# Turning q, k and x on TensorE, off-diagonal keys as tiles of their own, and a written-out order, in a local attention and low-rank mixer kernel

## The chip, the cores and the metric

The kernel runs on one core of one Trainium2 chip. The metric is the device time of the core in microseconds (us), of one launch. Engines are named as in the profile: PE is TensorE's matmul stream, PEld its weight loads, ACT is ScalarE, DVE is VectorE, POOL is GpSimd, and SP issues transfers. In the profile, L967 means line 967 of the kernel file.

## What is computed

There are 4 batches of 8 heads, 768 positions and 64 channels. Queries see the 8 first keys and the last 96 keys up to themselves, with a linear penalty on the distance; the heads' outputs, side by side, are x (768 by 512), which a low-rank mixing of the positions and an MLP then use:

```python
scores = scale * np.matmul(q, k.transpose(0, 1, 3, 2)) + bias   # local band and 8 global keys
a = np.exp(scores - max); a = a / (a.sum(-1) + 1e-09)
x = np.matmul(a, v)            # heads side by side: (4, 768, 512)
xt = x.transpose(0, 2, 1)
h = xt @ U @ V                 # U: 768 x 32, V: 32 x 768
u = x + h.transpose(0, 2, 1)
ch = np.maximum(u @ w_ch1, 0.0) @ w_ch2     # 512 -> 2048 -> 512
return u + ch
```

## The kernel before

**Units of work.** Heads go in pairs: pair p = 4b + hp holds heads 2hp and 2hp + 1 of batch b, so there are 16 pairs. `attention(p)` (L584) makes the tasks of one pair, `mlp(b)` (L952) those of one batch. Each task is one or a few instructions on one engine, with an estimated duration, the tasks that it needs, and the buffers that it takes and gives back. A planner (`Planner.run`, L159) walks through simulated time and always starts the ready task with the smallest priority number; the numbers are in a table `PRIO` or come from the place in the program. The result is one fixed order per engine. For a PE task that waits on another engine the planner keeps a `margin` (0.15 to 1.3 us) beyond the estimated latency.

**A pair.** Loads `lk`, `lq`, `lv` (L453, L457, L461; issued from POOL, cast to fp16 on the way; for pair 0, k and q come from SP in fp32 and are cast). For pairs 0 to 6 (`by_pe`) q and k are turned on PE by `TK` and `TQ` (`tr`, L600: 12 products of 64 columns each, with the identity, two column tiles at a time) and brought out of PSUM by `EK` and `EQ`. For pairs 7 to 15 `EK` and `EQ` are DMA transposes, issued from SP (`dtr`, L624). `KO` copies the 32 first keys of kT behind each block, so that a slice of 128 columns starting 32 further on is the off-diagonal key block; `VO` and `VG` build the fitting v blocks `vo` (shifted by 32 partitions, for most pairs by a transfer from SP, L651, then a copy on POOL, L368). `SB` puts the bias in PSUM (first batch only, L689: identity times a scaled bias), `S` makes the scores in products of 64 rows, two heads side by side in the array (L708), `EX` the exponential (L735), `MK` multiplies by a mask (batches 1 to 3), `PV` (L804, L805) multiplies by v, `RC` and `NM` divide (L839, L843), `XC` casts x to fp16 (L869).

**The mixing.** `UP` (`mixed`, L773) turns x by six products with the identity (L778) and makes U^T x by six products with u16 as the stationary operand (L788); `TE` copies the second to SBUF (L902), `HM` adds V times it in PSUM (L911; for batches 1 to 3 in two half arrays of 64 rows), and `E0`/`E1` bring out uT (L364). For pairs 12 to 15 (`XT`) x is turned by a DMA transpose (L880) instead of L778, and added on DVE. The other route, with x as the stationary operand (`xu`, tasks `XE` and `XU`), is in the code but no pair uses it.

**The MLP.** `M1a`/`M1b` (L967) are the first product: 16 units per batch, each 4 chunks (one per pair of the batch) by 2 halves of 384 columns; the first three chunks are `M1a`, the last `M1b`. The units go in turn through two pairs of PSUM banks, which `RL` (ReLU on ACT, L984) gives back. The second product uses seven products in place of eight (L1047, tasks `P1` to `P7`), with sums `PA`, `PB`, `TWa`, `TWb` on DVE; `RS` (L1035) adds the low-rank part in half arrays; `DI` to `DH` (L1060, L1083) add up, and SP stores (L1091).

**Order.** Attention of batch b + 1 runs between the products of batch b, in all phases. POOL issues all loads in its order, with at most 8 under way; SP issues stores, `vo` transfers and DMA transposes in its order. L1118 fills PE's idle time before the first M1 with products of zeros, to hold the clock.

Of the kernel before, what the change touches and what calls it, by code (L numbers as in the profile page):

```python
# [16 lines left out]
PE, ACT, DVE, POOL, SP = "PE", "ACT", "DVE", "POOL", "SP"  # L17


PRIO = {  # L20
# [244 lines left out]
def kernel(  # L265
# [13 lines left out]
    nc = tc.nc  # L279
# [888 lines left out]
```

## Time and profile before

| | |
|---|---|
| runs (us) | 232.76, 232.97, 234.19; median 232.97 |
| profiled execution: span, first to last instruction | 231.3 us |
| profiled execution: its own time | not given apart; the median of the runs lies 1.7 us above the span, the lowest run 1.5 us |
| first M1 product starts / last product's result reaches DVE | 35.09 us / 227.47 us |
| PE busy | 223.4 us (97%) |
| DVE, ACT, POOL busy | 153.1, 118.7, 90.2 us |
| granted TensorE clock | 1.000 |

A group line of the profile reads: line, engine, operation, what is written and read, shapes, count, then busy time, mean ns of one, and the idle time of the engine just before these instructions with what ended it. A matmul's mean is its length from issue to the end of its results, and they overlap: what one costs in a stream is the distance from one start to the next. The chain of waits is the work that ended last, followed back to the start.

### The profile page before, as it was taken

How to read it: one execution, taken by the hardware profiler on the slowest of the kernel's cores; microseconds unless marked ns; L12 is line 12 of the kernel's file. 1: busy time of each engine (PE TensorE's matmuls, PEld its weight loads, DVE VectorE, ACT ScalarE, POOL GpSimd, SP SyncE). 2: the span in 40 equal slices, each digit the busy share in tenths (PEclk: the TensorE clock that was granted, in tenths of full speed). 3: DMA queues.
4: the chain of work that ended last, by engine and by line, in shares of the span. 5: the costliest groups of instructions: out<-in, count | busy, mean ns of one | idle time of the engine just before them, and what ended most of it. 6: DMA issues, size and time to landing. Idle time of an engine off the chain costs nothing.

```text
span 231.3 us, 5732 instructions
## 1 busy us (share of the span) xinstructions
PE 223.4 (97%) x2402; PEld 158.3 (68%) x2402; DVE 153.1 (66%) x321; ACT 118.7 (51%) x161; POOL 90.2 (39%) x116
## 2 busy tenths in 40 slices
PE   7889999999999999999999999999999999999993
PEld 2556675565788885656678885666689875658882
DVE  6548772499987975375867785395888840626762
ACT  3576978878632446766652228868610025662000
POOL 9789968349929960264800911030100000000000
PEclk9999999999999999999999999999999999999999
DMA  7999999999999999992961995221020630000025
GB/s 169 162 163 150 156 189 211 207 188 166 167 157 160 175 166 235 219 123 22 130 56 41 162 162 173 56 41 30 15 22 17 157 136 4 0 0 3 0 84 191
DMA packets 89642, 26.96 MB, mean 117 GB/s; under 512 B 77040, under 2 KB 86640, under 8 KB 89616
## 3 DMA queue, kind: packets, MB, share of 16 engines
q0 software_dynamic: 63616, 13.24, 69.3%
q1 hardware_dynamic: 26000, 13.35, 27.3%
q8 instruction: 19, 0.31, 0.5%
q14 instruction: 7, 0.06, 0.1%
HBM read 27.46 MB, written 6.29 MB: 146 GB/s over the span
## 4 chain that ended last, share of the span: by engine, by line
PE 84%; POOL 7%; DMA 6%; issue 1%; ACT 0%; DVE 0%; POOLq 0%
PE ps L967 37%; PE ps L1047 33%; PE ps L708 4%; DMA vt<-in_v_dram 3%; DMA stgk<-in_k_dram 3%; PE ps L805 2%; PE ps L788 2%; POOL vo L368 2%; PE ps L804 2%; PE ps L1035 1%; POOL stgk L453 1%; POOL vt L461 1%; PE ps L778 1%; PE ps L911 1%; POOL stgq L453 1%
## 5 line engine op out<-in xcount | busy, mean ns | idle before, releaser
L967 PE MATMUL ps<-uT,w 128*128 128x384 f16 x512 | 88.1, 326 | 0.3 <-ACT uT L364 0.3
L967 PEld LDWEIGHTS <-w 128*128 128x128 f16 x512 | 48.1, 98 | 32.2 <-issue 1.0
L984 ACT ACTIVATE htr<-ps 128x768 f16<-128x768 f32 x64 | 51.9, 811 | 32.4 <-PE ps L967 32.2
L735 ACT ACTIVATE ep<-ps 128x1024 f16<-128x1024 f32 (+1 forms) x48 | 44.1, 952 | 16.0 <-PE ps L708 15.9
L1047 PEld LDWEIGHTS <-htr 128*128 128x128 f16 x384 | 36.1, 98 | 6.5 <-issue 2.0
L1047 PEld LDWEIGHTS <-sA 128*128 128x128 f16 x288 | 27.5, 98 | 3.8 <-issue 0.5
L461 POOL DMA_DIRECT2D vt<-in_v_dram x16 | 16.5, 1031 | 34.4 <-PE ps L805 27.9
L748 DVE TENSOR_TENSOR ep<-ep,mask 128x1024 f16<-128x1024 f16 x24 | 16.6, 691 | 16.4 <-ACT ep L735 16.4
L1060 DVE TENSOR_TENSOR x_sb<-ps,x_sb 128x256 f32<-128x256 f32 x48 | 19.9, 421 | 9.9 <-PE ps L1047 9.4
L1047 PE MATMUL ps<-w,htr 128*128 128x256 f16 x192 | 24.5, 273 | 0.0
L1047 PE MATMUL ps<-tB,htr 128*128 128x256 f16 x192 | 24.4, 273 | 0.0
L1047 PE MATMUL ps<-w,sA 128*128 128x256 f16 x192 | 24.4, 273 | 0.0
L368 POOL COPY vo<-vt 32x650 f16<-32x650 f16 x22 | 18.1, 823 | 9.5 <-DMA vt<-in_v_dram 8.9
L1001 DVE TENSOR_TENSOR sA<-htr 128x768 f16<-128x768 f16 x16 | 9.5, 594 | 18.3 <-ACT htr L984 18.1
L364 ACT ACTIVATE u<-ps 128x256 f32<-128x256 f32 x12 | 4.6, 384 | 29.7 <-PE ps L1047 29.7
L869 POOL CAST x<-x_sb 128x768 f16<-128x768 f32 x12 | 10.8, 906 | 22.7 <-DVE x_sb L843 12.8
L457 POOL DMA_DIRECT2D stgk<-in_k_dram x18 | 14.8, 834 | 3.8 <-PE ps L967 3.8
L708 PEld LDWEIGHTS <-kT 64*128 64x128 f16 x352 | 10.1, 94 | 8.9 <-issue 8.1
L457 POOL DMA_DIRECT2D stgq<-in_q_dram x18 | 14.9, 838 | 3.1 <-DMA w<-in_moe_w_ch_dram 3.1
L708 PE MATMUL ps<-qT,kT 64*128 64x128 f16 x352 | 15.6, 218 | 0.0
L843 DVE TENSOR_TENSOR x_sb<-ps,rcp 128x768 f32<-128x768 f32 x16 | 15.2, 956 | 0.4
L1060 DVE TENSOR_TENSOR u<-ps,u 128x256 f32<-128x256 f32 x24 | 10.0, 419 | 6.7 <-PE ps L1047 4.9
(78 smaller groups left out, 272.2 us busy)
## 6 DMA issues: line engine op xcount, KB each, us to landing
out_dram<-x_sb SPq DMA_DIRECT2D x23, 256.0 KB, 2.6
w<-in_moe_w_ch_dram POOLq DMA_DIRECT2D x8, 512.0 KB, 9.2
vt<-in_v_dram POOLq DMA_DIRECT2D x16, 192.0 KB, 7.1
stgk<-in_k_dram POOLq DMA_DIRECT2D x18, 96.0 KB, 6.8
stgq<-in_q_dram POOLq DMA_DIRECT2D x18, 96.0 KB, 6.2
vo<-vt SPq DMA_DIRECT2D x14, 121.9 KB, 4.9
stgk<-in_k_dram POOLq DMA_DIRECT2D x6, 192.0 KB, 6.7
stgq<-in_q_dram POOLq DMA_DIRECT2D x6, 192.0 KB, 6.6
```

Of the source, the lines that this page charges most:

```text
L368: nc.gpsimd.tensor_copy(dst, src)
L457: nc.gpsimd.dma_start(o[:, :, hi], src[b, h0 + hi].rearrange("(n p) d -> p n d", p=P))
L461: nc.gpsimd.dma_start(vt[gv.slot][:, :, :, 0:D], v[b, h0:h0 + 2].rearrange("h (n p) d -> p h n d", p=P),)
L708: nc.tensor.matmul(t[:, hi, j * P:(j + 1) * P], lhs, qt[r, i * P:(i + 1) * P], start=not biased, stop=True, skip_group_check=biased,)
L735: nc.scalar.activation(ep[gep.slot][:, :, lo:512], ps[:, gsc.slot:gsc.slot + 2, lo:512], AF.Exp, scale=qk_scale)
L748: nc.vector.tensor_tensor(ev, ev, mv, ALU.mult)
L843: nc.vector.tensor_tensor(xo, pvo()[:, :, :, 0:D], rcp[p % 2].unsqueeze(3).broadcast_to((P, 2, NB, D)), ALU.mult)
L869: (nc.vector if xe == DVE else nc.gpsimd).tensor_copy(x16[gx16.slot], src)
L967: nc.tensor.matmul(ps[:, g.slot + half, 0:HS], w1[:, dc, jt * P:(jt + 1) * P], ub[:, dc, half * HS:(half + 1) * HS], start=(dc == 0), stop ...
L984: nc.scalar.activation(htr[:, jt].rearrange("p (h c) -> p h c", h=2), ps[:, g.slot:g.slot + 2, 0:HS], AF.Relu)
L1047: nc.tensor.matmul(o, a[:, j, c0 + cols.start:c0 + cols.stop], bq[:, j], start=False, stop=(j == hj - 1), skip_group_check=True,)
L1060: return lambda: e.tensor_tensor(o(), x(), y(), ALU.add)
```

## The change

- **Order.** `PRIO`, the margins and the planner's choice go. `ORDER` lists all 967 tasks, and each engine runs its own in that order.
- **q and k.** Pairs 4 to 15 are all turned on PE by `flip`: 6 products of the full array per tensor. Their results are brought out by ACT or DVE (`EK`, `EQ`). No DMA transpose is left. Pairs 0 to 3 keep `tr`.
- **x.** All pairs turn x with the identity; the DMA transposes and DVE adds of pairs 12 to 15 go.
- **Low-rank products.** For pairs 4 to 15 `xu` is on: x is the stationary operand for both, the second moves 32 columns, `XE` copies the result four times side by side, `XU` turns it by one product.
- **Off-diagonal keys.** They get a tile of their own, `kO`, in place (global keys in rows 0 to 31 of each block, not behind the block); `vo` likewise needs no shift across partitions. `VC` and `VG` (mostly POOL; DVE for pairs 0, 1, 4; SP for 12, 13) replace `VO`. The bias is now a scaled identity (`ib`) times one relative-position tile.
- **Loads.** k is read by tokens in runs of 6 positions (before 2) for pairs 0 to 3; q and k of pairs 4 to 15 are two transfers each. U and V are loaded behind `KO1`. POOL's list begins lk1 lq1 lq3 lk3 lk2 lv0 lq2 lv1 lv3 lv2 lk4 lq4 lk5, then copies for pairs 3 and 2, then w1_0.
- **First MLP units.** Four units of batch 0 go in four steps (pairs 1, 0, 2, 3), each waiting for its pair alone.
- **Waits and engines.** ReLU and the sums wait only for those products of the batch before that read what they overwrite. Many copies get their engine from a table. A seven-product form of the first MLP product is in the code, with an empty list of units (`"Z": ()`), so it makes no task.

```diff
+CFG = {
+    "NU": (4, 5, 6, 7, 8, 9, 10, 11, 12, 13, 14, 15), "back": "KO1", "early": 4, "Z": (), "ZS": "DDDDDDDD", "ZR": "DDDDDDDD", "ZQ": "DDDDDDDD", "TE": "AADDAADADAAAAAAA", "XE": "DDDDDAADAAAAAAAA", "EK": "ADDDDDAAADADAAAD", "EQ": "DADAADAAAAADAAAA", "KO": "ADDDPPASPPSDAADD",
+    "HR": "RRFRRFFRRRFRRRRR", "RR": "RRRRRRRRRRRR", "IB": "ADADDDDA", "U16": "D", "VS": "PPDD", "C0": "DD",
+    "VO": "DDPPDPPPPPPPSSPP", "XC": "PDPDDAPDPPPPPPAA", "E": "AAAAAAAADDAAAADA",
...
-            s_ = src[b, h0:h0 + 2]
-            if src is q:
-                return dst, s_.rearrange("h (p n) d -> p h (n d)", n=NB)
-            return (
-                dst.rearrange("p h (m c) -> p h m c", m=NB // 2),
-                s_.rearrange("h (m p n) d -> p h m (n d)", m=NB // 2, n=2),
-            )
+            return dst, src[b, h0:h0 + 2].rearrange("h (p n) d -> p h (n d)", n=NB)
...
-        def dtr(dst, gd, stg, gs):
...
-                nc.sync.dma_start(
-                    o[:, :, 0:P] if dst is kT else o.rearrange("c (n p) -> c n p", n=NB),
-                    stg[gs.slot].rearrange("p a b -> p (a b)"), transpose=True,
-                )
+        def flip(g, stg, gs):
+            def go():
+                for n in range(NB):
+                    nc.tensor.matmul(
+                        ps16[:, g.slot, n * P:(n + 1) * P],
+                        stg[gs.slot].rearrange("p a b -> p (a b)")[:, n * P:(n + 1) * P],
+                        ident16, is_transpose=True, start=(n == 0), stop=(n == NB - 1),
+                    )
...
         def koff():
-            kt = kT[gkT.slot]
-            copy(ke, kt[:, 0:NB - 1, P:PK], kt[:, 0:1, 0:32].broadcast_to((P, NB - 1, 32)))
+            kt, ko = kT[gkT.slot], kO[gkT.slot]
+            copy(ke, ko[:, :, GP:P], kt[:, 0:NB - 1, GP:P])
+            copy(ke, ko[:, :, 0:GP], kt[:, 0:1, 0:GP].broadcast_to((P, NB - 1, GP)))
...
-            nc.sync.dma_start(vo[gv.slot][0:PO], vt[gv.slot][32:P, :, 0:NB - 1])
+            copy(vm, vo[gv.slot], vt[gv.slot][:, :, 0:NB - 1])
...
-                    nc.tensor.matmul(t[:, hi, lo:512], ident16, bb, start=True, stop=False, skip_group_check=True)
+                    nc.tensor.matmul(t[:, hi, lo:512], ib[:, h0 + hi], bb, start=True, stop=False, skip_group_check=True)
...
-                nc.vector.tensor_copy(xus[gxu.slot], ps[:, gx.slot, 384:384 + R].unsqueeze(1).broadcast_to((P, RG, R)))
+                copy(ENG[CFG["XE"][p]], xus[gxu.slot], ps[:, gx.slot, 384:384 + R].unsqueeze(1).broadcast_to((P, RG, R)))
...
+            steps = ((1,), (0,), (2,), (3,)) if b == 0 and n < CFG["early"] else ((0, 1, 2), (3,))
...
-            relus[jt] = add(ACT, 0.81, -10, relu, [Bt] + war, rel=[g], name=f"RL{b}.{n}")
+            relus[jt] = [add(ACT, 0.81, relu, [Bt] + war(*((1, 7) if jt < hj else (2, 4))), rel=[g], name=f"RL{b}.{n}")]
```

The part of `ORDER` around the first MLP units, all engines mixed:

```
... VC2 VG2 u16 PV2 UP1 EX3.1 w1_0 vs2 TE1 RC2 NM2 PV3.0 TK4 EK4 vs0 HM1 mask1 E01 PV3.1 RC3.1 NH3.1 XC0 UP0 TQ4
XC2 w1_1 RC3.0 TE0 NH3.0 KO4 UP2 EQ4 HM0 E00 PV3.2 TE2 S4.2 EX4.2 HM2 E02 RC3.2 UP3.0 lq5 UP3.1 NH3.2 UP3.2 NM3
TE3 TD0 S4.0 HM3 E13 E03 M1a0.3 lv4 M1c0.3 w1_2 w1_3 EX4.1 M1d0.3 M1b0.3 RL0.3 M1a0.2 mask3 M1c0.2 w2_2 mask0 TK5 ...
```

More of the change, by code (lines that the diff above doesn't have):

```diff
@@ L17 @@
 PE, ACT, DVE, POOL, SP = "PE", "ACT", "DVE", "POOL", "SP"
-PRIO = {
[71 rows of a table removed]
+ENG = {"A": ACT, "D": DVE, "P": POOL, "S": SP}
+ORDER = """
+wz iota vz relf rel3 bias6 ones3 bias1 bias4 bias0 lk0 Ck0 TK0 bias3 lq0 Cq0 bias5 SB0.2 TQ0 EQ0 lk1 SB0.0 ones1
+ones0 TK1 EK1 KO1 bias7 lq1 TQ1 EK0 KO0 S0.2 S0.0 SB0.1 S0.1 back bias2 lq3 EQ1 ones2 lk3 TK3 EK3 EX0.0 lk2 lv0
+EX0.1 lq2 lv1 lv3 lv2 EX0.2 SB1.2 TK2 S1.2 EX1.2 SB1.0 S1.0 lk4 EX1.0 lq4 SB1.1 mixl lk5 EK2 S1.1 EX1.1 VC0 VG0 TQ3
+EQ3 KO2 TQ2 EQ2 PV0 RC0 SB2.2 S2.2 VC3 EX2.2 SB2.1 SB2.0 S2.0 S2.1 EX2.0 VC1 VG1 PV1 KO3 EX2.1 NM0 VG3 RC1 NM1 SB3.2
@@ new lines @@
+S3.2 SB3.0 S3.0 SB3.1 S3.1 XC1 EX3.2 EX3.0 VC2 VG2 u16 PV2 UP1 EX3.1 w1_0 vs2 TE1 RC2 NM2 PV3.0 TK4 EK4 vs0 HM1
+mask1 E01 PV3.1 RC3.1 NH3.1 XC0 UP0 TQ4 XC2 w1_1 RC3.0 TE0 NH3.0 KO4 UP2 EQ4 HM0 E00 PV3.2 TE2 S4.2 EX4.2 HM2 E02
+RC3.2 UP3.0 lq5 UP3.1 NH3.2 UP3.2 NM3 TE3 TD0 S4.0 HM3 E13 E03 M1a0.3 lv4 M1c0.3 w1_2 w1_3 EX4.1 M1d0.3 M1b0.3 RL0.3
+M1a0.2 mask3 M1c0.2 w2_2 mask0 TK5 EK5 KO5 w2_0 w2_1 MK4.1 M1d0.2 M1b0.2 w2_3 RL0.2 M1a0.0 M1c0.0 EX4.0 M1d0.0 TQ5
+EQ5 M1b0.0 RL0.0 M1a0.7 M1b0.7 S5.0 mask2 M1a0.6 EX5.0 RL0.7 M1b0.6 RL0.6 lk6 MK4.0 EX5.1 VC4 VG4 MK4.2 PV4 M1a0.11
@@ L119, with __init__ @@
     LANES = 8
-    def __init__(self, counts, dma_rate, hold, switch):
+    def __init__(self, counts, dma_rate, switch):
         self.tasks, self.names = [], {}
@@ L124, in __init__ @@
         self.held = []
-        self.until = None
-        self.dma_rate, self.hold, self.switch = dma_rate, hold, switch
+        self.dma_rate, self.switch = dma_rate, switch
     def add(self, name, *a, **k):
@@ L144, in pick @@
                 best = (f, i)
+        if best is None:
+            raise RuntimeError("no room for " + g.kind)
         return best
@@ L157, in unused, with run @@
         return best and best[1]
-    def run(self):
-        engines = (PE, ACT, DVE, POOL, SP)
-        clock = {PE: 0.0, ACT: 2.0, DVE: 0.7, POOL: 1.2, SP: 0.7}
+    def run(self, names):
+        if sorted(names) != sorted(self.names):
+            raise RuntimeError("order and tasks differ")
+        clock = {PE: 0.0, ACT: 2.0, DVE: 0.7, POOL: 0.75, SP: 0.7}
         lanes = {POOL: [0.0] * self.LANES, SP: [0.0] * self.LANES}
         mode = 0
-        dma_free = {POOL: 0.0, SP: 0.0}
-        waits = {}
-        users = {}
-        for t in self.tasks:
-            before = t.deps + ([t.after] if t.after is not None else [])
-            waits[t] = len(before)
-            for d in before:
-                users.setdefault(d, []).append(t)
-        live = {e: {} for e in engines}
-        def release(t):
+        dma_free = {POOL: 4.1, SP: 0.0}
+        for t in (self.names[n] for n in names):
@@ L175, in release @@
             r = 0.0
             for d in t.deps:
-                lat = d.lat + (t.margin if t.eng == PE and d.eng != PE else 0.0)
-                if t.eng == d.eng and d.size == 0.0:
-                    lat = 0.0
-                r = max(r, d.end + lat)
-            if t.after is not None:
-                r = max(r, t.after.start + t.after.dur)
-            live[t.eng][t] = r
-        for t in self.tasks:
-            if not waits[t]:
-                release(t)
-        order = []
-        while len(order) < len(self.tasks) and not (self.until and self.names[self.until].end):
-            best = None
-            for e in engines:
-                ready = []
-                for t, r in live[e].items():
-                    r = max([r] + [g.read for g in t.bw] + [g.written for g in t.br])
-                    taken = []
-                    for g in t.acq:
-                        if g.slot is None:
-                            got = self.pick(g, taken)
-                            if got is None:
-                                break
-                            r = max(r, got[0])
-                            taken.append((g.kind, got[1]))
-                    else:
-                        if t.size:
-                            r = max(r, lanes[e][t.parts - 1])
-                        ready.append((max(r, clock[e]), t.prio, t))
-                if not ready:
-                    continue
-                first = min(r[0] for r in ready)
-                s, _, t = min((r for r in ready if r[0] <= first + self.hold[e]), key=lambda r: (r[1], r[0]))
-                if e == PE and t.mode != mode:
-                    s = max(s, clock[e] + self.switch)
-                if best is None or s < best[0]:
-                    best = (s, t)
-            if best is None:
-                raise RuntimeError("stuck: " + " ".join(t.name for e in engines for t in live[e]))
-            s, t = best
-            del live[t.eng][t]
@@ new lines, in run @@
+                r = max(r, d.end + (0.0 if t.eng == d.eng and d.size == 0.0 else d.lat))
+            r = max([r] + [g.read for g in t.bw] + [g.written for g in t.br])
+            for g in t.acq:
+                if g.slot is None:
+                    f, g.slot = self.pick(g)
+                    r = max(r, f)
+                    for i in range(g.slot, g.slot + g.n):
+                        self.free[g.kind][i] = 1e9
+            if t.size:
+                r = max(r, lanes[t.eng][t.parts - 1])
@@ L219, in run @@
+            s = max(r, clock[t.eng])
+            if t.eng == PE and t.mode != mode:
+                s = max(s, clock[PE] + self.switch)
+                mode = t.mode
+            for g in t.acq:
+                if g.since is None:
+                    g.since = s
             t.start, t.end = s, s + t.dur
             clock[t.eng] = t.end
-            if t.eng == PE:
-                mode = t.mode
             if t.size:
@@ L237, in run @@
                     ring.append(t.end)
-            for g in t.acq:
-                if g.slot is None:
-                    g.slot = self.pick(g)[1]
-                    g.since = s
-                    for i in range(g.slot, g.slot + g.n):
-                        self.free[g.kind][i] = 1e9
             for g in t.bw:
@@ L254, in run @@
                         self.held.append((g.kind, i, g.since, g.free_at))
-            order.append(t)
-            for u in users.get(t, ()):
-                waits[u] -= 1
-                if not waits[u]:
-                    release(u)
-        order.sort(key=lambda t: t.start)
-        return order
+        return sorted((self.names[n] for n in names), key=lambda t: t.start)
 @with_exitstack
@@ L355 @@
     pl = Planner(
-        {"sq": N_STG, "sk": N_STG, "v": N_V, "kT": N_QK, "qT": N_QK, "ep": N_EP, "x16": N_X16, "u2": N_U, "u3": N_U, "xT": N_XT, "xu": 2, "ps": 8},
+        {"sq": N_STG, "sk": N_STG, "v": N_V, "kT": N_QK, "qT": N_QK, "ep": N_EP, "x16": N_X16, "u2": N_U, "u3": N_U, "xu": 2, "ps": 8},
         dma_rate=1.0,
-        hold={PE: 0.0, ACT: 0.15, DVE: 0.15, POOL: 0.3, SP: 0.0},
         switch=0.09,
@@ new lines, in one @@
+                e = ENG[CFG["C0"][i]]
+                return add(e, {ACT: 0.81, DVE: 0.6, POOL: 0.9}[e], lambda: copy(e, dst[g.slot], stg32[i]), [t], acq=[g], name=f"C{nm}0")
+            ldur, parts, size = (0.8, 1, 1.0) if p in by_pe else (1.68, 2, 1.35)
+            return add(POOL, ldur, ld(dst, src, g), acq=[g], size=size, parts=parts, name=f"l{nm}{p}")
+        tk = one(k, stgk, gk, "k", 0)
+        tq = one(q, stgq, gq, "q", 1)
+        tv = add(POOL, 1.04, ldv, [c_ones[p]] if p < N_V else [], acq=[gv], size=1.75, name=f"lv{p}")
@@ L656, in attention @@
-        vm = CFG.get("VO", "DPSSSSSSSSSSSSSS")[p]
-        if vm != "S":
-            ve = {"D": DVE, "P": POOL, "A": ACT}[vm]
-            def vo_d(c):
-                return lambda: copy(ve, vo[gv.slot][c:c + 32], vt[gv.slot][c + 32:c + 64, :, 0:NB - 1])
-            VO = [
-                add(ve, {POOL: 0.76, DVE: 0.8, ACT: 0.8}[ve], base + 4, vo_d(c), [tv], name=f"VO{p}.{c // 32}") for c in range(0, PO, 32)
-            ]
-        else:
-            VO = [add(SP, 0.6, base + 4, vo_sp, [tv], size=0.6, name=f"VO{p}")]
@@ new lines, in flip, with flat, arrange @@
+            return go
+        def flat(g, eng, dst):
+            return lambda: copy(eng, dst(), ps16[:, g.slot, 0:S])
+        def arrange(x, stg, gs, ld, gt, dst, i):
+            g = Group("ps", among=A1)
+            first_ = p in by_pe
+            t = add(
+                PE, 0.37 if first_ else 0.34, (tr if first_ else flip)(g, stg, gs), [ld, c_id16],
+                lat=0.3, acq=[g], rel=[gs], mode=3 if first_ else 0, name=f"T{x}{p}",
+            )
+            e = ENG[CFG["E" + x][p]]
+            return add(
+                e, 0.83 if e == ACT else 0.95, (evac if first_ else flat)(g, e, dst), [t], acq=[gt], rel=[g],
+                name=f"E{x}{p}",
+            )
@@ new lines, in attention @@
+        EK = arrange("K", stgk, gk, tk, gkT, kcols, 0)
+        EQ = arrange("Q", stgq, gq, tq, gqT, lambda: qT[gqT.slot], 1)
+        ke = ENG[CFG["KO"][p]]
+        def koff():
+            kt, ko = kT[gkT.slot], kO[gkT.slot]
+            copy(ke, ko[:, :, GP:P], kt[:, 0:NB - 1, GP:P])
+            copy(ke, ko[:, :, 0:GP], kt[:, 0:1, 0:GP].broadcast_to((P, NB - 1, GP)))
+        KO = add(ke, {ACT: 0.92, DVE: 0.9 if first else 0.6, POOL: 0.95, SP: 0.2}[ke], koff, [EK], size=0.8 if ke == SP else 0.0, parts=2, name=f"KO{p}")
@@ new lines, in attention, with vo_keys, vo_globals @@
+        vm = ENG[CFG["VO"][p]]
+        def vo_keys():
+            copy(vm, vo[gv.slot], vt[gv.slot][:, :, 0:NB - 1])
+        def vo_globals():
+            o, i = vo[gv.slot][0:GP], vt[gv.slot][0:GP, :, 0:1]
+            if vm == SP:
+                for h in range(2):
+                    copy(vm, o[:, h], i[:, h].broadcast_to((GP, NB - 1, DP)))
+            else:
+                copy(vm, o, i.broadcast_to((GP, 2, NB - 1, DP)))
+        VC = add(vm, {POOL: 0.75, DVE: 0.45 if first else 0.35, ACT: 0.75, SP: 0.1}[vm], vo_keys, [tv], size=0.5 if vm == SP else 0.0, name=f"VC{p}")
@@ L671, in attention @@
+        VO = [add(vm, {POOL: 0.75, DVE: 0.45 if first else 0.35, ACT: 0.75, SP: 0.2}[vm], vo_globals, [VC], size=0.4 if vm == SP else 0.0, parts=2, name=f"VG{p}")]
         geps, MKs = [], []
@@ L761, in attention @@
         gpv = Group("ps", 4 if split else 1, n=2, among=A2)
-        xdma = p in CFG.get("XT", ())
-        xu = p in CFG.get("NU", ()) and not xdma
-        gx16 = Group("x16", 2 if xdma else 1)
+        xu = p in CFG["NU"]
+        gx16 = Group("x16")
         gx = Group("ps", 1, n=2, among=A2)
@@ L855, in attention @@
             PV = add(
-                PE, 0.68, base + 16, pv_all, MKs + VO, margin=mg, lat=0.3, acq=[gpv], rel=geps + [gv], name=f"PV{p}"
+                PE, 0.68, pv_all, MKs + VO, lat=0.3, acq=[gpv], rel=geps + [gv], name=f"PV{p}"
             )
-            RC = add(DVE, 0.23, base + 20, rc, [PV], name=f"RC{p}")
-            NM = add(DVE, 0.96, base + 21, norm, [RC] + xw, rel=[gpv], name=f"NM{p}")
-            xe = DVE if last else POOL
-            if first and CFG.get("XC", "PPP")[p] != "P":
-                xe = {"A": ACT, "D": DVE}[CFG["XC"][p]]
+            RC = add(DVE, 0.23, rc, [PV], name=f"RC{p}")
+            NM = add(DVE, 0.96, norm, [RC] + xw, rel=[gpv], name=f"NM{p}")
+            xe = ENG[CFG["XC"][p]]
             def cast():
@@ L1112 @@
         mlp(b)
-    order = pl.run()
+    c_back.deps.append(pl.names[CFG["back"]])
+    order = pl.run(ORDER)
     def idle(n, width, bank):
```

491 lines of the change are left out of this document (263 added, 228 removed), and 71 rows, old and new, of the table PRIO.

## The prediction

> **What bounds the kernel now.** I read the page first (busy shares, slices, chain), then PE's waits, then the chain in order of time, then PE's timeline before the first MLP product, then POOL's and DVE's there.
>
> ```profile
> span 231.3 us, 5732 instructions
> PE 223.4 (97%) x2402; PEld 158.3 (68%) x2402; DVE 153.1 (66%) x321; ACT 118.7 (51%) x161; POOL 90.2 (39%) x116
> DMA  7999999999999999992961995221020630000025
> PE 84%; POOL 7%; DMA 6%; issue 1%; ACT 0%; DVE 0%; POOLq 0%
> ```
>
> ```profile
> PE ps L600 <- DMA stgk<-in_k_dram: 1.7, 2, 1.1
> PE ps L1118 <- POOL zero L379: 1.3, 1, 1.3
> PE ps L778 <- ACT uT L364: 0.4, 1, 0.4
> PE ps L967 <- ACT uT L364: 0.3, 1, 0.3
> ```
>
> PE waits for almost nothing: 3.7 us in all. But L1118 is filler, and it hides waits. The chain, in order of time:
>
> ```profile
> 26.41 6.84 DMA stgk<-in_k_dram
> 33.29 0.53 PE ps L600 x12
> ...
> 35.16 2.71 PE ps L967 x16
> 37.87 0.33 PE ps L708 x8
> ...
> 40.90 0.50 PE ps L708 x14
> ...
> 85.08 0.34 PE ps L778 x6
> 85.42 0.34 PE ps L788 x6
> ...
> 106.72 2.60 PE ps L967 x16
> ...
> 227.47 0.42 DVE x_sb L1060
> ```
>
> Two stretches with different limits. Until 35.1 us (35.09 in the timeline) the end is set by loads and the chain of small copies: the DMA row is at 9 from its second slice, and the last step before the first MLP product is a load of 6.84 us (k of pair 5, which PE must turn first). From 35.1 to 227.5 the chain is PE alone, with one gap of 0.5 us at 88 us: 192.4 us of work, in which only PE's instructions count. Then come 3.8 us of last sum and store. DVE, ACT, POOL and DMA, however busy, cost nothing there as long as they deliver in time.
>
> Prices on PE, from the distances between starts in its timeline after 35 us: 384 columns 0.1604 us (M1); 256 columns 0.1087; 128 columns, full array 0.056 (L778, L788: 0.34 for 6); L805/L804 with 65 columns 0.0305; scores 0.0277 each. Every group of half-array or column-tiled products (L708, L1035, L600, L911 by 64 rows) costs 0.11 us on entering and 0.11 on leaving: 8 scores take 0.33, 14 take 0.50, so 0.028 each and 0.11 over; and the 16 M1 products behind a group take 2.71, those with none 2.60. There are 37 such groups after 35 us.
>
> **The sum for the PE stretch (after the first M1 product starts).**
> - *q and k.* Before, 9 pairs were turned by DMA and 3 by tiles (L600), of which only the 24 products of pair 6 come after 35 us. After, pairs 5 to 15 come there: 22 turns x 6 x 0.056 = 7.39, less 24 x 0.029 = 0.70: **+6.7 us**. `flip` uses the full array, so I price it as L778.
> - *x and the low-rank products*, pairs 4 to 15. Before: 72 L788 and 48 L778 = 6.71. After: 72 x 0.056 for the turn, 72 of 32 columns, 12 `XU` x 0.056. No row moves 32 columns. From above: 0.0305 (65 columns, as many weights), giving 6.90; from below: that row scaled to 32 columns, 0.015, giving 5.8. I take the upper end, whose weight load is the same: **+0.2**, at best -0.9.
> - *Groups by tile.* Counting the order's PE tasks after the first M1 task by the same rule gives 26 groups, against 37, since `S`, `HM` and `RS` stand together more often and no L600 is left: 11 x 0.22 = **-2.4**.
> - *`HM`.* Three pairs (5, 6, 10) now use the full array: 2 x 0.16 in place of 2 x 0.073 each: **+0.5**. *Scores:* S4.0 (14) moves ahead of M1: **-0.4**.
> - *Same on PE:* scores with `kO`, `PV`, bias products, M1 in four steps, `RS`, P1 to P7: same counts and shapes.
>
> Sum +4.6: 192.4 becomes **197.0**.
>
> Here the trace meets a rule that speaks against the change. L600's products, which carry the transpose flag, start 0.029 us apart, though each lasts 236 ns by its group line; the full-array L778 lasts 219 ns and starts every 56 ns. The Trainium skill, TensorE: Matmul & The Clock Gate, Part 4, gives about 275 ns for one 128 by 128 transpose in a kernel and says that this mode does not hold the clock up. If 275 ns were the distance between starts, the 132 turns would cost 36 us and not 7.4; the trace disagrees for the tiled form, and the granted clock is 1.000 throughout. The same page (Part 1) puts the least distance between starts at about 25 ns, for 32 columns; by it the low-rank step would be -0.2 us in place of +0.2, an estimate that no run here shows.
>
> **The sum for the start.** What must be there before M1 is all of batch 0's attention, and w1_0.
> - *Loads.* Before, the queue brought pairs 0 to 3, w1_0, w1_1 and most of pair 4 before k of pair 5 landed at 33.25. After, w1_0 is behind k4, q4, k5 only, and TK5 stands behind six M1 steps: w1_1 and v4 leave the path. Pace: k of pair 1 at 7.2 us (TK1's start), v of pair 1 at 15.4, six items on: 1.37 each, less for k in longer runs; I take 1.25 for pairs 1 to 3. The 7th item, q2, lands at 7.4 + 6 x 1.25 = 14.9, the 10th, v2, near 19, k4/q4/k5 near 24, and w1_0, twice or thrice an item, near 27.
> - *DVE*, whose queue ends last. q2 at 14.9, TQ2 0.46, EQ2 0.96 and two hand-overs of 0.2: 16.7. Behind it in the order until TE3: RC and NM of pairs 0 to 2 (3 x 1.19), VC1+VG1 0.8, KO3 0.7, XC1 0.78, u16 0.74, vs2 0.34, EK4 0.96, three RC/NH 1.8, TE2 and TE3 0.57, NM3 0.96 = 11.2. That ends at 27.9; HM3 and the hand-over 0.3: **M1 starts at 28.2**. Durations from DVE's groups (956, 229, 778, 742, 283 ns); VC and the wider KO are bounded by the 317 ns of 160 columns and the 956 of 768.
> - *ACT*: 12 EX (0.81 and 1.02) that run from 10.3 to about 23, then TE, E0, EQ4, EX4 to 28.2: E02 and E13 are due at the third and fourth M1 step, 28.9 and 29.2. It fits by half a us. The early steps are what make it fit; with the old `M1a` the start would be E02's, some 0.4 later.
> - Lower end 27 (w1_0); upper end 30.6, if DVE idles for 2.4 us over k3, k2 and v0 or KO4 (POOL, behind w1_1's issue) holds S4.2, which stands ahead of HM2 on PE.
>
> The start is **6.9 us** earlier.
>
> **What lies beside PE, costed at nothing.**
> - 18 more copies out of PSUM and 10 `XE`, 12 `TE`, 4 `KO`, 3 `XC` on ACT: about +21 us, 119 to 140 of 229 (61%). DVE gains 7 (EK/EQ) and loses TE, the xT adds and the wide biases: about 155. Cover: PE's dense M1 and P products.
> - `VC`/`VG` on POOL (22 of 0.75 in place of 22 copies at 0.82): same. `VO`'s transfers and 22 transposes leave SP, so stores are behind less; the last store has no such neighbour before either, so the tail stays 3.8.
> - Pairs 4 to 6 now load q and k as two transfers each (POOL 1.66 in place of 0.84): +5 us of issue on a queue that idles 1 to 12 us at a time after 40 us. U and V wait for KO1 (10 us), needed at u16 (21 us).
> - New waits: KO of pairs 7 and 10 and VC/VG of 12 and 13 are transfers from SP now, queued behind stores; `vo`'s took 4.9 us to land, and S7, S10, PV12 and PV13 stand several P or M1 products later, which is their cover; without it PE would wait up to those 4.9 us. XU waits for XE: rival 2.
> - Looser waits of ReLU and sums: no PE wait there now, so no gain.
>
> **Together.** 28.2 + 197.0 + 3.8 = 229.0 us of span against 231.3; 1.6 us around it (1.5 to 1.7 by the runs shown): 230.6; the 0.5 us gap at 88 us is a wait of M1 for uT that the new order gives room (S8.2 stands between HM7 and M1), of which I count 0.1 to 0.2. **230.4 us**, 1.1% faster. What a measurement of this kernel can tell from no change is about 1% (2.3 us, so 230.6 and 235.3 are the borders).
>
> **Rivals.**
> 1. *The start stays with the loads.* For: DMA at 9 in every slice to 100 us; runs of one position now from k4 on, which pairs 7 to 15 landed at a like 6.4 us but at a loaded queue. Against: w1_0 has 1.2 us of room. If the start is 30.6: 232.8, no change.
> 2. *Slower: the turn of the low-rank result waits.* `XU` stands 0.87 us (one P product) behind `UP` in most places; XE, on ACT for 10 of 12, needs 0.3 and two hand-overs of 0.2, but ACT works in order, and an EX (1.02) or RL (0.81) ahead of it makes PE wait some 0.5 to 0.8 with all products behind `XU` stuck. Likewise M1 behind EX and RL, with the margins gone. Twelve turns at 0.5 = 6.0: 236.4. It decides from 0.41 us a turn (4.9 us). For: ACT near 87% in the M1 phases. Against: now not one wait of that kind in the trace, with M1's own ReLU as tight.
> 3. *`flip` is not a plain product.* If a turn with the flag drains PE as a tiled group does, 16 places (several stand together) x 0.22 = 3.6: 234.0, no change. The rows can't exclude it: L600 is tiled and flagged at once.
>
> **How the numbers follow.** Forecast 0.58, with its own range 228.0 to 231.6, of which 0.08 lies above 230.6; rival 1 0.20; rival 2 0.13; rival 3 0.09. Faster: 0.50; within 1%: 0.08 + 0.20 + 0.09 = 0.37; slower: 0.13. The range reaches from 227.8 (start at 27, low-rank step at its lower end, with a rest kept) to 234.2 (rival 3), and leaves out rival 2 and a little of the low side.
>
> **What would show it.** Right: first M1 product at 27.5 to 29; the stretch from there to the last product about 197; 132 turns 56 ns apart; fewer than 30 tiled groups; PE's waits after the start below 1 us; ACT near 140. Wrong: PE waits on `xus` or `tmp` (rival 2), starts of `flip` with 0.2 over (rival 3), a wait for w or stgk ahead of M1 (rival 1).

## The result, and the profile after

| | before | after |
|---|---|---|
| median (us) | 233.2 (232.76 to 234.19, 4 runs) | 229.87 (229.02 to 231.71, 4 runs) |
| ratio, 95% interval | | 0.9859 [0.9824, 0.9895] |
| profiled execution: span / own time | 231.3 | 229.9 / 231.71 |
| first M1 product starts | 35.09 | 29.40 |
| first M1 to the last product's end (the stretch) | 192.34 | 197.40 |
| from there to the end (the tail) | 3.82 | 3.12 |

The change made the kernel 1.4% faster; forecast were 230.4 us and 1.1%. The profiled execution of after is the slowest of its four: the other three have spans of 227.2 to 228.1 us. A trace of the same kernel on another chip (`c0_after_again` below) had a span of 228.7, with the start at 29.50, a stretch of 196.12 and a tail of 3.12; it is used beside this one. Ratios and their intervals leave out the few executions more than 1.5% above the fastest of their kernel, which the medians keep.

The page after (the span, the busy shares, the DMA row of the slices, and the shares of the chain by engine):

```profile
span 229.9 us, 5824 instructions
PE 222.9 (97%) x2455; PEld 161.7 (70%) x2455; DVE 151.8 (66%) x314; ACT 137.4 (60%) x202; POOL 97.4 (42%) x129
DMA  7999899999998999949596173510000043000015
PE 89%; DMA 6%; POOL 2%; DVE 1%; issue 0%; POOLq 0%; DVEq 0%
```

PE is as full as before, with 53 more instructions. ACT has 137.4 us (forecast 140), DVE 151.8 (155): both near what the sums of copies said; ACT is not among the shares of the chain, and DVE has 1% of it. PE's waits, complete, and the chain from 25 to 37 us:

```profile
PE ps L485 <- DMA stgq<-in_q_dram: 1.3, 1, 1.3
PE ps L1081 <- POOL zero L314: 1.3, 1, 1.3
PE ps L504 <- DMA stgq<-in_q_dram: 1.1, 1, 1.1
```

```profile
25.59 0.69 POOL w L413
26.28 0.84 POOL kO L303 x2
27.12 0.75 POOL stgq L382
27.87 6.60 DMA stgq<-in_q_dram
34.48 0.14 issue
34.61 0.49 PE ps L504 x6
35.10 1.62 PE ps L836 x10
```

The first two waits lie before the first MLP product. The third is new: the turn of q of pair 5 stands early in PE's order, and its load is issued from POOL only at 27.1 us, behind w1_1's issue and `KO4`. In PE's timeline (start, length, what; L504 is `flip`, L836 M1):

```profile
29.40 2.12 PE L836 MATMUL ps<-uT,w 128*128 128x384 f16 x12
31.36 0.50 PE L504 MATMUL ps<-ident,stgk 128*128 128x128 f16 x6
31.70 1.79 PE L836 MATMUL ps<-uT,w 128*128 128x384 f16 x10
34.61 0.49 PE L504 MATMUL ps<-ident,stgq 128*128 128x128 f16 x6 [1.12 <-DMA stgq<-in_q_dram]
34.94 1.79 PE L836 MATMUL ps<-uT,w 128*128 128x384 f16 x10
```

Six turns take 0.34 us from start to start (31.36 to 31.70, 34.61 to 34.94): 0.056 each, nothing on entering or leaving. From the start of each product to the start of the next, PE's stretch divides as follows (us):

| | before | after | forecast of the difference |
|---|---|---|---|
| turns of q and k | 0.92 | 7.46 | +6.7 |
| turn of x, low-rank products | 6.71 | 6.54 (3.97 + 1.91 + 0.67) | +0.2 |
| M1 | 85.72 | 84.34, and 1.28 around the wait for q of pair 5 | |
| second MLP product, `RS` | 78.81 | 78.32 | |
| scores, `PV`, `HM` | 20.19 | 19.48 | |
| groups by tile (count) | 37 | 26 | 37 to 26 |

The last three rows of times together are 2.58 lower; forecast for groups, scores and `HM` were -2.4, -0.4 and +0.5, so -2.3. That the two agree hides two differences. First, a group costs less than forecast: an M1 product ahead of one takes 258 ns to the next start in place of 162, in both kernels, so entering costs 0.096 us; leaving costs as much, which is in the row of the group's last product. That makes 0.19 a group and 2.1 for 11. Second, M1's row of before holds a wait of 0.5 us for uT, which is gone after (the next start was due at 87.98):

```profile
87.66 0.50 PE L967 MATMUL ps<-uT,w 128*128 128x384 f16 x2
88.47 1.79 PE L967 MATMUL ps<-uT,w 128*128 128x384 f16 x10 [0.31 <-ACT uT L364]
```

With -2.1 for the groups, -0.5 for this wait, -0.4 for the scores and +0.5 for `HM` the sum is -2.5, against -2.6 in the rows.

### The profile page after: what moved, and what is told of

Same layout as the page of the kernel before. It is cut to its first block, busy times and chain, and to the rows that moved or that the text cites. A ratio compares the mean times of both kernels' runs of the same rounds, so it can differ in the third digit from the quotient of the medians.

```text
span 229.9 us, 5824 instructions
## 1 busy us (share of the span) xinstructions
PE 222.9 (97%) x2455; PEld 161.7 (70%) x2455; DVE 151.8 (66%) x314; ACT 137.4 (60%) x202; POOL 97.4 (42%) x129
## 4 chain that ended last, share of the span: by engine, by line
PE 89%; DMA 6%; POOL 2%; DVE 1%; issue 0%; POOLq 0%; DVEq 0%
PE ps L836 35%; PE ps L1011 32%; DMA stgq<-in_q_dram 6%; PE ps L591 5%; PE ps L504 3%; PE ps L686 3%; PE ps L659 2%; PE ps L685 2%; PE ps L572 2%; PE ps L780 1%; PE ps L1001 1%; DVE x_sb L1024 1%; PE ps L485 1%; PE ps L664 1%; POOL kO L303 0%; POOL x L748 0%
## 5 line engine op out<-in xcount | busy, mean ns | idle before, releaser
L836 PE MATMUL ps<-uT,w 128*128 128x384 f16 x512 | 87.5, 326 | 0.1
L836 PEld LDWEIGHTS <-w 128*128 128x128 f16 x512 | 48.4, 98 | 31.1 <-issue 0.2
L748 POOL CAST x<-x_sb 128x768 f16<-128x768 f32 x9 | 8.2, 910 | 63.7 <-DVE x_sb L724 55.6
L1024 DVE TENSOR_TENSOR x_sb<-ps,x_sb 128x256 f32<-128x256 f32 x48 | 19.4, 417 | 4.8 <-PE ps L1011 4.2
L382 POOL DMA_DIRECT2D stgk<-in_k_dram x24 | 20.1, 858 | 4.4 <-DMA w<-in_moe_w_ch_dram 2.8
L382 POOL DMA_DIRECT2D stgq<-in_q_dram x24 | 20.0, 852 | 3.5 <-DMA w<-in_moe_w_ch_dram 3.5
L631 DVE TENSOR_TENSOR ep<-ep,mask 128x1024 f16<-128x1024 f16 x24 | 17.6, 754 | 0.8 <-ACT ep L618 0.6
L303 POOL COPY vo<-vt 128x660 f16<-128x660 f16 (+1 forms) x22 | 17.3, 789 | 0.5
L591 PE MATMUL ps<-qT,kT 64*128 64x128 f16 x192 | 14.2, 217 | 0.0
L686 PE MATMUL ps<-vt,ep 128*128 128x65 f16 x192 | 13.6, 193 | 0.0
L686 PEld LDWEIGHTS <-ep 128*128 128x128 f16 x192 | 12.5, 97 | 1.0
## 6 DMA issues: line engine op xcount, KB each, us to landing
w<-in_moe_w_ch_dram POOLq DMA_DIRECT2D x8, 512.0 KB, 11.2
```

Source lines behind the costliest of these rows:

```text
L303: nc.gpsimd.tensor_copy(dst, src)
L382: nc.gpsimd.dma_start(o[:, i], src[b, h0 + i].rearrange("(n p) d -> p n d", p=P))
L591: nc.tensor.matmul(t[:, hi, j * P:(j + 1) * P], lhs, qt[r, i * P:(i + 1) * P], start=not biased, stop=True, skip_group_check=biased,)
L631: nc.vector.tensor_tensor(ev, ev, mv, ALU.mult)
L686: nc.tensor.matmul(o, e[:, hi, (j + 1) * P:(j + 2) * P], vv[:, hi, i, 0:D1], start=(i == 0), stop=True)
L836: nc.tensor.matmul(ps[:, g.slot + half, 0:HS], w1[:, dc, jt * P:(jt + 1) * P], ub[:, dc, half * HS:(half + 1) * HS], start=(dc == flat[0]) ...
```

## Experiments

All are the changed kernel with the edit shown; where tasks go, their names go from `ORDER` too. The line numbers of each move by a few. Ratios are to the kernel before on the same chip. "M1" is the start of the first M1 product.

**q of pair 5 later.** Is the wait at 33.5 us worth its 1.1 us?

```diff
-M1d0.0 TQ5 EQ5 M1b0.0 RL0.0 M1a0.7 M1b0.7 S5.0 mask2 M1a0.6 EX5.0 RL0.7 M1b0.6 RL0.6
+M1d0.0 M1b0.0 RL0.0 M1a0.7 TQ5 EQ5 M1b0.7 RL0.7 mask2 M1a0.6 S5.0 EX5.0 M1b0.6 RL0.6
```

> The changed kernel with the turn of pair 5's q (TQ5, EQ5) and its scores (S5.0) one M1 unit later on PE. Theory (PE alone sets the end after the first M1 product, so a wait of PE counts whole): the wait of 1.1 to 1.3 us for q of pair 5 near 33.4 us goes, and the time falls by 1.1 us against the changed kernel (ratio to the kernel before about 0.981). Rival (the loads bound this stretch anyway): the wait turns up a unit later, on w or on stgq, and the time stays within 0.3 us of the changed kernel.

Measured: 230.34 us, 0.9880 [0.9833, 0.9927]; the wait is gone (one of 0.3 us for `ep` from ACT came in), M1 29.07, stretch 196.56. The median did not fall. The reason is in the other traces: with the order as it was, `c0_after_again` and the two runs below have no such wait either, and one further down has 0.5 us. It comes and goes with the landing of that load, and the profiled execution of after happened to have it.

**Without the early steps.** The first four units of batch 0 in two steps, as all others.

```diff
-"early": 4
+"early": 0
```

> The changed kernel with the first four M1 units in two steps (three pairs, then the last) as before, at the same place in the order. Theory: the copy E02 ends at 29.35 us and M1 starts at 29.40, so waiting for it costs PE 0.1 us at most, and the time stays within 0.3 us. Rival (the early steps are what lets M1 start): M1 starts 0.4 us later or more, and the time rises by as much.

Measured: 229.50 us, 0.9835 [0.9803, 0.9866]; M1 28.35, stretch 196.10. Not slower: the early steps are worth nothing here, where the prediction gave them 0.4 us.

**Without the x-stationary products.** `XE` and `XU` go; U is the stationary operand again.

```diff
-"NU": (4, 5, 6, 7, 8, 9, 10, 11, 12, 13, 14, 15)
+"NU": ()
```

> The changed kernel with the low-rank products of all pairs by the old route (u16 stationary, 128 columns moved, no XE and XU). Theory: PE pays 12 x (6 x (0.056 - 0.027) - 0.055) = 1.45 us more after the start and the time rises by 1.4 us. Rival (the turn of the small result makes PE wait, which eats its gain): the time stays within 0.4 us or falls, with fewer gaps on PE.

Measured: 231.24 us, 0.9895 [0.9864, 0.9925]; stretch 197.47. The turn of x and the low-rank products take 4.02 + 4.02 = 8.04 us, against 6.54 in after: 1.5 in the rows, and 1.3 in the stretch (196.2 is the mean of the six traces with these products, all turns on PE by full products, and no wait on q of pair 5). The median is 0.9 and 1.7 us above those of the two runs before it, on the same chip. This part helps, and no wait of PE on `xus` is in any trace with it.

**The last turns of q and k by DMA again.** Pairs 12 to 15 first, then 8 to 15; the transposes of pairs 14 and 15 are moved on SP's list to just before and after the last stores of batch 1.

```diff
+"DT": (12, 13, 14, 15)
+if p in CFG["DT"]:
+    EK, EQ = dtr("K", kT, gkT, stgk, gk, tk), dtr("Q", qT, gqT, stgq, gq, tq)
...
```

> The changed kernel with q and k of pairs 12 to 15 turned by DMA transposes from SP again; the rest as it is. Theory: 8 turns x 6 x 0.056 = 2.7 us leave PE, DMA has room after 100 us, and the time falls by 2.7 us. Rival (the transposes land too late or hold up SP's stores and the copies behind them, and PE waits): the time stays within 0.5 us of the changed kernel or rises, with PE waits on kT or qT.

Measured: 229.22 us, 0.9818 [0.9786, 0.9851]; turns 4.78 (2.66 less), but stretch 195.57, only 0.6 less than the 196.2. DVE's and PE's timelines of this run say where 1 us went:

```profile
140.75 0.96 DVE L735 TENSOR_TENSOR x_sb<-ps,rcp 128x768 f32<-128x768 f32 x1 [1.95 <-DMA out_dram<-x_sb]
```

```profile
141.76 0.23 PE L602 MATMUL ps<-qT,kO 64*128 64x128 f16 x2 [0.95 <-DVE x_sb L735]
```

`NM12` waits for the last store of batch 1, which it overwrites in `x_sb`, and the scores of pair 14 wait for the PSUM that `NM12` gives back. That store landed 4.6 us after its issue, beside the transposes of pair 15 (3.1 in `c0_after_again`); that the transposes delayed it is likely but not shown, since in the next run it took 2.4 beside the same two. Waits of 0.3 us for a part of w1 and 0.2 for `u` are new as well; the last half us is not accounted for.

> The changed kernel with q and k of pairs 8 to 15 turned by DMA transposes from SP. Theory (a turn's price on PE counts only if the other way delivers in time): 16 x 0.336 = 5.4 us leave PE, but SP's queue and the stores that PSUM buffers hang on are held up by 1.3 us of issue for each, and waits on PE give back 2 us or more, as the one of 1.0 us in the run with pairs 12 to 15: net -1 to -3.5 us against the changed kernel. Rival (transposes are as good as free beside PE): -5 us.

Measured: 233.05 us, 0.9973 [0.9935, 1.0011]; turns 2.12 (5.3 less), stretch 198.93. PE's waits:

```profile
PE ps L602 <- DMA qT<-stgq: 3.6, 3, 2.4
PE ps L602 <- DMA kO<-kT: 1.9, 1, 1.9
```

The products saved are paid back in waits of the scores for transfers, 5.5 us in all, and in a slower clock. The row of the granted clock on the page dips behind the wait of 2.4 us, and the 16 M1 products that follow it take 4.39 us, start to start, where 16 take 2.60 elsewhere:

```profile
PEclk9999999999999988999999999999999999999999
```

```profile
84.52 0.23 PE L602 MATMUL ps<-qT,kO 64*128 64x128 f16 x2 [2.40 <-DMA qT<-stgq]
84.85 4.45 PE L847 MATMUL ps<-uT,w 128*128 128x384 f16 x16
```

The clock was at 0.50 for 3.4 us there, which is another 1.7 us. All ten executions have a mean clock of 0.993 or less; the six of the yardstick below have 0.999 or 1.000. So the whole gain of the change is gone, and some 1.7 us of that is the clock. In this order, which was not laid out for them, the turns on PE are worth their 5.3 us: they take the transfers off PE's path. How the DMA form would do in an order of its own was not tried.

**The yardstick.** The changed kernel again, without an edit.

> The changed kernel itself again, as the yardstick of this group. Theory: the first M1 product starts between 28.3 and 29.4 us, as in the runs so far, and the wait for q of pair 5 comes and goes with the loads; the PE stretch without it is 196.1 us and the tail 3.1. Median near 229.9 us.

Measured: 230.25 us, 0.9863 [0.9825, 0.9901]. Over the eight traces with its order of loads and copies and three buffers M1 starts at 28.35 to 29.50, mean 29.0: a difference of less than 1 us between the starts of two traces says nothing.

**v's off-diagonal blocks of pairs 0 and 1 on POOL.** What is the start's gain made of?

```diff
-"VO": "DDPPDPPPPPPPSSPP"
+"VO": "PPPPDPPPPPPPSSPP"
```

> The changed kernel with the off-diagonal v blocks of pairs 0 and 1 copied by POOL and not by DVE, as for most other pairs. Theory (the start is a chain over DVE's and POOL's small copies and the load issue behind them): four copies of 0.75 us stand in POOL's queue ahead of the copies of pairs 2 and 3 and of w1_0, and M1 starts 1.5 to 3 us later, the PE stretch the same. Rival (the loads alone set the start): POOL has room, and M1 starts within 0.5 us of the yardstick.

Measured: 235.81 us, 1.0117 [1.0060, 1.0175]; M1 33.96, stretch 196.11. One line of PE's waits holds nearly all of it:

```profile
PE ps L684 <- POOL vo L302: 4.3, 1, 4.3
```

The direction was right and the size, 4.9 us, twice the middle of what was expected: on POOL these copies stand behind a long row of loads. Part of it is the clock again, which was at 0.50 for 3.4 us from 18.9 us on, right behind this wait:

```profile
PEclk9997999999999999999999999999999999999999
```

With these copies on POOL the start is within 1.1 us of the kernel before, and the changed kernel is slower than it, by the stretch.

**Four staging buffers.** POOL's fourth load of k waits 1.61 us for one of three buffers (at 4.9 us in after), which the prediction did not see.

```diff
-N_STG, N_V, N_QK, N_EP, N_X16, N_U = 3, 4, 3, 6, 3, 2
+N_STG, N_V, N_QK, N_EP, N_X16, N_U = 4, 4, 3, 6, 3, 2
```

> The changed kernel with four staging buffers for q and k in place of three. In the changed kernel POOL's queue stands 1.6 us at 4.9 us, since the load of pair 2's k needs a buffer that the turn of an earlier pair must give back, with all later loads behind it. Theory (that stall moves the loads of pairs 2 and 3, and with them the start): M1 starts 0.5 to 1.5 us earlier and the time falls by as much. Rival (the loads are served at the rate of the DMA engines, which are busy anyway): M1 starts within 0.4 us of the yardstick.

Measured: 229.35 us, 0.9831 [0.9793, 0.9868], beside the yardstick's 0.9863 on that chip; M1 27.93, stretch 195.94, the stall gone. POOL now waits 1.33 and 1.02 us for loads of v further on instead. A gain of 0.9 us in the median, with intervals that overlap: not settled.

> Four staging buffers as in the run before, and DMA transposes from SP for q and k of pairs 12 to 14 only; pair 15 stays on PE. Theory: the start stays near 28 us; 6 x 0.336 = 2.0 us leave PE, and the wait of 1.0 us that the run with pairs 12 to 15 had at S14 is gone, since no transposes of pair 15 run beside the last stores of batch 1: stretch 194.0 us, time 2 us under the four-buffer run (about 227.4). Rival (the transposes of pairs 12 to 14 delay those stores as well): a wait of 0.5 us or more at S14 stays, and the time is within 1 us of the four-buffer run.

Four buffers, and pairs 12 to 14 by DMA: 229.26 us, 0.9769 [0.9719, 0.9818]; M1 28.67, stretch 195.55. The forecast of 194.0 and of 2 us in the time missed: the wait of 1.0 us at the scores of pair 14 is gone, as said, but of the 2.0 us of products taken off PE only 0.4 show against four buffers alone, and none in the median. The lower ratio comes from the kernel before, which had a median of 234.21 in this group of runs and 233.28 in the one before it.

> The kernel with four buffers and DMA transposes for pairs 12 to 14, and in the start: v of pair 2 loaded and its off-diagonal blocks copied ahead of those of pair 3, and the cast u16 moved ahead of RC1 on DVE, where DVE stood 0.8 to 1.0 us waiting for pair 1's products. Theory (DVE's queue sets the start): M1 starts 0.5 to 1.0 us earlier, and the time falls by as much. Rival (U lands too late for the earlier place, or POOL's copies of pair 3 come late now): DVE waits there, and M1 starts at the same time or later.

The same with pair 2's v ahead of pair 3's, on DVE's and POOL's lists and in the loads, and u16 ahead of `RC1`: 228.75 us, 0.9767 [0.9721, 0.9813]; M1 28.83, not earlier, so this theory of the start fell. Its stretch is 194.54, with none of the waits for q, `qT` and `x_sb` that the one before shows (0.5, 0.3 and 0.2 us); the two medians differ by less than their spread. It has the lowest median of all, 0.6 us below four buffers alone, with ranges that overlap.

**w1_0 and w1_1 ahead of k and q of pair 4.** In `ORDER` only the place of two loads changes. The filler changes with it: the number of products of zeros follows from the planner's estimate of PE's idle time, and before the first M1 product it is 78 here, 19 in the yardstick.

```diff
-S1.0 lk4 EX1.0 lq4 ... EX3.1 w1_0 vs2 ... XC2 w1_1 RC3.0
+S1.0 w1_0 w1_1 lk4 EX1.0 lq4 ... EX3.1 vs2 ... XC2 RC3.0
```

> The changed kernel with w1_0 and w1_1 issued on POOL ahead of lk4, lq4 and lk5 (in place of behind them), nothing else moved on any engine. Theory (the start gains because the loads that are not needed for the first MLP product, or are needed last, no longer stand ahead of those that feed PE's fixed order): k4 and q4 land some 2 to 5 us later, TK4 and TQ4 stand ahead of HM1 and HM0 on PE, so the first M1 product starts at 31 to 34 us in place of 28.35 to 29.5, the stretch stays at 195.5 to 197.5, and the median is 232 to 235. Rival (the start is set by DVE's and ACT's work whatever the loads do): the start stays within 28.3 to 29.6 and the median at 229.5 to 230.5.

Measured: 233.71 us, 0.9995 [0.9963, 1.0027]; M1 31.24, 2.2 later than the mean, stretch 196.48. The size came out as expected, by another way: PE's waits show none for k or q of pair 4. POOL's timeline, first of this run and then of the yardstick:

```profile
11.63 1.53 POOL L412 DMA_DIRECT2D w<-in_moe_w_ch_dram  x2
...
16.16 0.83 POOL L381 DMA_DIRECT2D stgq<-in_q_dram  x1 [0.54 <-DMA vt<-in_v_dram]
18.04 1.75 POOL L381 DMA_DIRECT2D stgk<-in_k_dram  x2 [1.05 <-PE ps L590]
19.79 3.57 POOL L302 COPY vo<-vt 128x660 f16<-128x660 f16 x4
```

```profile
15.88 1.70 POOL L382 DMA_DIRECT2D stgk<-in_k_dram  x2
17.50 3.08 POOL L303 COPY vo<-vt 128x660 f16<-128x660 f16 x4
20.54 0.76 POOL L413 DMA_DIRECT2D w<-in_moe_w_ch_dram  x1
```

The two issues of w1 (1.53 us) and the waits of the issues behind them (0.54 and 1.05) move POOL's `vo` copies of pairs 3 and 2: they start 2.3 us later and end at 23.36 in place of 20.58. `PV2` needs them. In PE's timeline it stands right behind 56 products of the filler:

```profile
20.83 3.30 PE L1080 MATMUL ps<-zero 128*128 128x128 f16 x56
23.97 0.23 PE L685 MATMUL ps<-vt,ep 128*128 128x65 f16 x2
```

In the yardstick `PV2` starts at 21.79. DVE then sits 2.07 us idle before the sum of pair 2:

```profile
24.84 0.23 DVE L719 RECIPROCAL rcp<-ps 128x12 f32<-128x12 f32 x1 [2.07 <-PE ps L685]
```

So what passes the delay on is, for 1.6 of these 2.2 us, POOL's queue (23.36 less 21.79), and not the landing of a load that PE needs; the other 0.6, from the copies' end to `PV2`, is covered by the filler, and what it would be without that was not tried. By the ratios the run is 3.1 us slower than the yardstick; 2.2 is the start, 0.6 the tail of this trace (3.71), 0.3 the stretch.

**Turns by column tiles.** Rival 3's price, measured: each full-array turn of pairs 4 to 15 as two products of 64 columns.

```diff
-    ps16[:, g.slot, n * P:(n + 1) * P], stg[...][:, n * P:(n + 1) * P], ident16, is_transpose=True
+    for hi in range(2):
+        ps16[64 * hi:64 * hi + 64, g.slot, n * P:(n + 1) * P], stg[...][:, n * P + 64 * hi:n * P + 64 * hi + 64], ident16, is_transpose=True
```

> The changed kernel with each of the 132 full-array turns of q and k after the first MLP product (and those of pair 4 before it) made as two products of 64 columns of weights into the two column tiles (the form of the turns of pairs 0 to 3); results, places and order stay. Theory (a full-array turn is a plain product of 55.7 ns, a tiled one costs 29 ns per product and about 0.19 to 0.22 us per group for entering and leaving): 22 x (12 x 0.029 - 6 x 0.0557) = +0.3, and 15 more groups by tile in the order (41 in place of 26) at 0.19 to 0.22 = +2.8 to 3.3, so the turns' row or the rows next to them grow by 3.1 to 3.6 us, the stretch to 199 to 200, the median to 232.5 to 234. Rival (the tiled turn costs nothing more than the full one, the group price is that of the scores alone): stretch +0.3 at most, median 229.5 to 230.6.

Measured: 233.15 us, 0.9992 [0.9966, 1.0019]; stretch 199.23, 3.1 above the yardstick, turns 9.22 in place of 7.46 and the rest in the rows beside them; 41 groups, if turns with `RS` right behind them count as two. As the theory had it. By its lengths the group line shows nothing of this (222 ns each, against 219 in after):

```profile
L505 PE MATMUL ps<-ident,stgk 128*64 128x128 f16 x144 | 6.1, 222 | 0.0
```

```profile
L504 PE MATMUL ps<-ident,stgk 128*128 128x128 f16 x72 | 5.8, 219 | 0.0
```

## Why the prediction was right, step by step

- **The start: right in kind, mis-sized by 0.8 us.** Forecast 28.2; 29.40 in after, 29.0 as a mean, 6.1 us earlier than before in place of 6.9. DVE's list ends last, as said, and q of pair 2 left it at 16.97 (forecast 16.7). The term that failed is its idle time, put at nothing up to TE3:

```profile
19.85 0.23 DVE L720 RECIPROCAL rcp<-ps 128x12 f32<-128x12 f32 x1 [0.82 <-PE ps L686]
...
26.62 0.29 DVE L299 CAST tmp<-ps 128x128 f16<-128x128 f32 x1 [0.43 <-PE ps L669]
27.17 0.18 DVE L701 RECIPROCAL rcp<-ps 128x4 f32<-128x4 f32 x1 [0.26 <-PE ps L686]
```

  That is 1.5 us in which DVE waits for `PV` and `UP`. Without these waits the list took 10.6 us to the end of TE3, where the sum had 11.2, so part of it was made good. The early steps, credited with 0.4, are worth nothing (`"early": 0`).
- **What carries the start.** The prediction put it on the order of the loads and on DVE's list. Both bear on it: w1 ahead costs 2.2 us, the copies of v for two pairs off DVE cost 4.9, each with a share that is the filler's or the clock's. But the first works through POOL's queue, which the prediction costed as issue time after 40 us and, for the start, only in its upper end (`KO4`); the 1.6 us stall for a staging buffer was missed with it. How much of the 35.09 us of before was its wait for k of pair 5 was not tried on the kernel before, but its trace sets a bound. M1's first products need uT of three pairs, its last steps that of the fourth, and DVE brought these out at 32.55 and 33.52:

```profile
31.59 0.96 DVE L366 CAST uT<-ps 128x768 f16<-128x768 f32 x1
32.58 0.94 DVE L366 CAST uT<-ps 128x768 f16<-128x768 f32 x1
```

  With k of pair 5 out of the way M1 could have started no earlier than about 32.6, 2.5 us sooner. So at most 2.5 of the 6.1 us are that load and what stood behind it; the rest is the earlier end of batch 0's own loads, copies and products, which no run on the kernel before divides further.
- **The stretch: forecast +4.6; +3.8 without the wait for q of pair 5, +5.1 with it.** The turns are +6.5 (6.7), the low-rank step -0.2 (+0.2, the upper bound taken), the rest -2.6 (-2.3). In the rest, the groups were priced at 0.22 and cost 0.19, so -2.1 in place of -2.4, and the whole 0.5 us wait for uT went, of which 0.1 to 0.2 was counted. The upper bound of the low-rank step was the wrong choice: a product of 32 columns is followed by the next start after 26.6 ns, between the bounds of 15 and 30.5. The Trainium skill, TensorE: Matmul & The Clock Gate, Part 1, has about 25 ns, and its -0.2 for this step is what came out.
- **The transpose flag.** 132 turns took 7.46 us in after, 56 ns each, at a granted clock of 1.000. One turn lasts 219 ns by its group line, and they overlap. The Trainium skill, TensorE: Matmul & The Clock Gate, Part 4, has about 275 ns for one in a kernel; here that is no distance between starts.
- **The tail** was to stay at 3.8; it is 3.1 to 3.3 in all traces of the new order but one (3.71). Whether the order or the execution does it is open, with one trace of before.
- **The signs.** Four of the six held in the profiled execution. The start, to be at 27.5 to 29, was 29.40, and PE's waits behind it, to be below 1 us, were 1.1; over eight traces the start is 29.0, and `c0_after_again` has no such wait.
- **Rivals.** The first (start at 30.6) fell in size: no trace with this order of loads and copies starts after 29.50, while the run with w1 ahead, at 31.24, shows that the start does hang on where loads stand among POOL's tasks. The second (PE waits for the turn of the low-rank result) fell: no such wait, and undoing the x-stationary products costs 1.3 us. The third (the flag drains PE) fell: `flip` costs what a plain product costs, and the tiled form has the price, 3.1 us by experiment where the rival gave 3.6.
- **Together.** The start was put 0.8 too early, the stretch 0.9 and the tail 0.7 too long, and the time around the span 0.2 too short; that these errors came to only 0.5 together was luck. 29.0 + 196.1 + 3.1 = 228.2 agrees with the span of the run at the median (228.1), and 1.8 around it gives 229.9.

## What to carry to other kernels

When one engine is dense, price a change there by distances between starts, tile groups included, and look elsewhere for the stretch in which that engine waits: here it lost 3.8 us where it was full and gained 6.1 where it was not. Before the dense part, write out every in-order queue that feeds it, the issuing engine's too: an issue placed ahead of a copy delays that copy by its own time and by what the issues between the two wait for. A transfer taken off a loaded path can be worth more than the products that replace it: so it was with pairs 8 to 15 together, but not with the last three or four pairs alone. Look at the row of the granted clock behind every long wait of PE, and at the filler that hides one. One trace of a load's landing is no evidence on a wait of 1 us.

## What the runs showed of the chip

- Full-array products of 128 columns with the transpose flag start 55.7 ns apart, without it 55.8 (`e3_no_xu`, L657); no gap stands ahead of either or behind it. A group by half array or column tile costs 0.096 us on entering and about as much on leaving, in after and in before, under the 0.11 each that the prediction read from the merged lines. The Trainium skill, TensorEngine Tiling (Array Packing), Key Properties, says that a change of tiling mode drains the engine; the runs put 0.19 us on it.
- The granted clock fell behind PE's long waits: after 2.40 us (`e5_dma_turn_8to15`) and 4.27 us (`e6_vo01_pool`) it was 0.50 for 3.4 us, which costs 1.7 us of PE's work. After waits of up to 1.94 us in these traces it stayed at 1.00.
- DMA transposes landed 2.7 to 7.6 us after their issue in `e5_dma_turn_8to15`; for one of 6.9 us, which landed at 84.48 us, the scores of its pair waited 2.4 us.
